# Another cost model in a kernel's planner, and value copies moved from DMA to GpSimd

## The chip, the core and the metric

One core of a Trainium2 chip runs the kernel as one program. The metric is device time in microseconds (us), median of the timed runs. An eight-byte-float input is read as pairs of 32-bit words; nothing is computed on the host.

## The reference, cut to what matters

Windowed attention with 32 global tokens (4 batches, 8 heads, 512 local tokens, head size 64, window 32), whose output is laid out as 2176 rows of 512, and then two feed-forward networks (512 to 2048 to 512) one after the other:

```python
s_ll = np.where(np.abs(pos[:, None] - pos[None, :]) <= 32, scale * q_l @ k_l.T, -1e9)
out_l = sm(concat([scale * q_l @ k_g.T, s_ll])) @ concat([v_g, v_l])
out_g = sm(scale * q_g @ concat([k_g, k_l]).T) @ concat([v_g, v_l])
x = rows(concat([out_g, out_l]))        # (2176, 512)
h = x @ w_in;   x = (h * cos(h)) @ w_out        # first network
h = relu(x @ w2_in);   out = (h * h) @ w2_out   # second network
```

The four weight matrices are eight-byte floats.

## The kernel before, in words

**Attention.** The work goes by 16 head pairs and 8 groups of two pairs (a group is half a batch). For a pair TensorE transposes keys and queries (`tk`, `tq`), forms windowed scores (`s`, L365), ScalarE takes the exponent (`pt`, L390), GpSimd gathers the part for the global keys (`pg`, L409), TensorE transposes the weights (`tw`, L418, and `tg`, L423) and multiplies them with the values (`o`, L441 and L456). Windows of 128 keys start at every 64th position, so the values are held twice: `va` as loaded, and `vb`, the same rows shifted by 64 partitions. In `copy_v` (L248) two DMAs per group on the queue of SyncE (SP), each of 64 partitions of 1024 numbers, make `vb` from `va`. All loads of attention stand on that queue too (`kn`, `qn`, `va`, `vgz`, `kgn`, `qgn`).

**Networks.** Each network is cut into blocks of the tokens (384, 384 or 320 columns twice) and into quarters of the hidden layer; a step is one block with one pair of hidden chunks. The first product of a step uses seven products of half-size blocks instead of eight (`PROD`, banks `ha`, `hb`, `he`), with sums of the inputs (`xr`, L681) and of the weights (`ws`, L160). Each operand is split in a high and a low part (`hi` by ScalarE, `lo` by L147 on GpSimd or VectorE), and three matmuls stand for one exact product. The weights are turned from eight-byte to four-byte floats first: two ScalarE or GpSimd instructions (L115 or L117, and L122), a shift and an OR on VectorE (L126, L131), a sum on GpSimd (L138). The second product of a step (`y`, L906) is added to the output tile `xt` by VectorE (L917), in its first round moved by VectorE or ScalarE (L921, L919). Inputs of the first product are stored to DRAM (`xs_B`, `xs_T`, L704) and read back (L709) for the later quarters.

**Planner.** Nothing above is issued in the order of the code. Every piece is an `Op` with the engines that can do it and a duration on each; the function walks over all `Op`s in a simulated time, gives each engine the ready one that is due first (`latest`), and emits the program in the order of the simulated starts. So a duration in the table is an instruction's place in the program. Ops on `Q` are DMAs of SP's queue. Each engine runs what it was given in that order, and one that waits holds all behind it. `opVG` makes an Op that VectorE or GpSimd can do; `port` names engines that the plan lets run only in turns; `beside[0]` is set from the first network's later preparations on; `made_early` are the preparations that may run beside attention; `nxt` counts the products that have been placed.

The lines that make a DMA and a shared operation in the plan:

```python
def opQ(kb, fn, *needs):
    return Op({"Q": kb / 330.0}, lambda e: fn(), *needs, lag=2.0)
def opVG(n, fn, *needs):
    o = Op({"G": d_g2(n), "V": d_v2(n)}, lambda e: fn(V if e == "V" else G), *needs)
    o.port = "GV"
```

Of the kernel before, what the change touches and what calls it, by code (L numbers as in the profile page):

```python
# [27 lines left out]
def kernel(  # L28
# [14 lines left out]
    nc = tc.nc  # L43
# [65 lines left out]
    def conv_u(q, m, c, on):  # L109
        t = raw[q, m, c]  # L110
        u = conv_to(q, m, c)
        tmp[q, m, c, 0] = u.bitcast(U32)
        h = t[:, :, 1].bitcast(F32)
        if on == "A":
            A.activation(u, h, AF.Copy, scale=2.0**-112)  # L115
        else:
            G.tensor_scalar(u, h, 2.0**-112, 1.0, op0=ALU.mult, op1=ALU.mult)  # L117
# [6 lines left out]
    def conv_v(q, m, c):  # L124
        u = tmp[q, m, c, 0]
        V.tensor_scalar(u, u, 3, None, op0=ALU.logical_shift_left)  # L126
# [118 lines left out]
                v_l[b, g, P * c - SG + r0 : P * c - SG + r1].rearrange("h p d -> p h d"),  # L245
            )

    def copy_v(gi):  # L248
        va, vb = VA[gi % 2], VB[gi % 2]
        nc.sync.dma_start(vb[0:64], va[64:128, 0:4])  # L250
        nc.sync.dma_start(vb[64:128], va[0:64, 1:5])

    def load_vg(b):

# [359 lines left out]
    load_qk("k", 1, 0, 2)  # L614
    load_qk("q", 1, 0, 2)
    load_vg(0)
    copy_v(0)
    load_qk("k", 1, 2, 2)
    load_qk("q", 1, 2, 2)
    for t in KT:  # L620
# [130 lines left out]
    def opV(d, fn, *needs):  # L751
        return Op({"V": d}, lambda e: fn(), *needs)

    def opG(d, fn, *needs):
        return Op({"G": d}, lambda e: fn(), *needs)

    def opVG(n, fn, *needs):
        o = Op({"G": d_g2(n), "V": d_v2(n)}, lambda e: fn(V if e == "V" else G), *needs)
        o.port = "GV"
        return o  # L760
# [1 line left out]
    beside = [False]  # L762

    def opQ(kb, fn, *needs):
        return Op({"Q": kb / 330.0}, lambda e: fn(), *needs, lag=2.0)

    class Ring:

# [304 lines left out]
    def conv(q, m, c):  # L1073
        j, free = raw_ring.next()
        k, cfree = cc_ring.next()
        RJ[q, m, c] = j, k
        ld = opQ(525.0, lambda: conv_load(q, m, c), *free)
        ld.lag += 0.0 if beside[0] else 4.0
        ld.raw = True
        if m:  # L1080
            w, wfree = wf1_ring.next()
            WJ[q, c] = w
        else:
            wfree = w_free["wf0"]
        u = Op({"G": 0.66, "A": 0.67}, lambda e: conv_u(q, m, c, e), ld, *wfree)
        s = opA(0.67, lambda: conv_s(q, m, c), ld, *cfree)
        v = opV(0.42, lambda: conv_v(q, m, c), u)
        o = opV(0.69, lambda: conv_o(q, m, c), s, u)
        v.port = o.port = "GV"
        raw_ring.free[j] = [o]  # L1090
        end = opG(1.25, lambda: conv_c(q, m, c), v, o)
        cc_ring.free[k] = [end]
        return end

# [40 lines left out]
    def opP(m, d, fn, *needs):  # L1135
# [3 lines left out]
        att_pe.append(o)  # L1139
        return o  # L1140

    def soft(fn, *needs):

        o = Op({"N": 0.0}, lambda e: fn(), *needs)
        o.soft = True
        return o
# [6 lines left out]
        for i in range(2):  # L1153
            q_in["k", 2 * g + i], q_in["q", 2 * g + i] = given(tk[i]), given(tq[i])
    q_in["v", 0] = given(12.0)
    q_in["vb", 0] = given(17.0)
    q_in["vg", 0] = given(15.0)
    q_in["kg", 0], q_in["qg", 0] = given(3.9), given(8.6)
    tring, TBANK = Ring(4), (0, 1, 2, 5)
# [15 lines left out]
    def load_kq(gi):  # L1175

        for w, free in (("k", kn_free), ("q", qn_free)):
            o = Op({"Q": 2.7}, lambda e, w=w: load_qk(w, gi), *free.get(gi - 2, []), lag=3.0)
            q_in[w, 2 * gi] = q_in[w, 2 * gi + 1] = o

    def load_vals(gi):
        o = q_in["v", gi] = Op({"Q": 3.1}, lambda e: load_v(gi), *va_free.get(gi - 2, []), lag=3.0)
        q_in["vb", gi] = Op({"Q": 1.2}, lambda e: copy_v(gi), o, *vb_free.get(gi - 2, []), lag=3.0)

    def load_vgz(b):
        q_in["vg", b] = Op({"Q": 1.9}, lambda e: load_vg(b), *vg_free.get(b - 2, []), lag=3.0)

    def tbank(*needs):
        k, free = tring.next()
# [223 lines left out]
    def join(*ops):  # L1413
        return Op({"N": 0.0}, lambda e: None, *ops)

    ORDER = (
# [12 lines left out]
    def att_graph():  # L1429
        mode[0] = "T"  # L1430
        for b in range(B):
            kg_ready[b], qg_ready[b] = join(), join()
        kg_b((0, 1))
        k_tr(0)
        q_tr(0)
        load_vals(1)
        load_vgz(1)
        for b in range(1, B):
            for w, dst, src in (("kg", kgn, k_g), ("qg", qgn, q_g)):
                q_in[w, b] = Op(  # L1440
                    {"Q": 0.45}, lambda e, b=b, dst=dst, src=src: load_small(dst, src, b), lag=3.0
                )
        for what in ORDER.split():
            name, i = what.split(":")
            DO[name](int(i))
# [86 lines left out]
    for o in allops:  # L1532
        set_latest(o)
    for o in made_early:
        o.latest -= 30
        if "Q" in o.on and hasattr(o, "raw"):
            o.latest -= 30

# [5 lines left out]
    def release(o):  # L1544
        if o.soft:
            o.at = max([x.start for x in o.needs]) + 1e-4
        else:
            p = "P" in o.on
            o.at = max([x.end + x.lag + (0.0 if p and x.eng == "P" else SEM) for x in o.needs], default=o.at)
        for e in o.on:  # L1550
            ready[e].append(o)

# [5 lines left out]
    def best(e):  # L1558
# [28 lines left out]
        if e in "VAG":  # L1587
# [20 lines left out]
                        return (min(g, min([max(f, y.at) for y in rest if y.att], default=g)), None) if g < t + 0.4 else (t, o)  # L1608
            if o.att:
                return t, o  # L1610
        if e in o.on and len(o.on) > 1 and e == "V" and o.latest > t + BIAS:
            can = [x for x in can if len(x.on) == 1 or x.latest <= t + BIAS]
            if not can:
                rest = [max(f, x.at) for x in ready[e] if len(x.on) == 1]
                g = max(min(free_at[x] for x in o.on if x != "V"), t)
                if g <= t + 0.5 or (rest and min(rest) < t + 0.3):
                    return (g + 1e-3, None) if not rest else (max(min(rest), t + 1e-3), None)
                return t, o
            o = min(can, key=lambda o: (o.latest, o.key))
        return t, o  # L1620

    port = [0.0]
    BIAS, LOOK, drift = -100, 1.0, [0.0]
    count = len(allops)
    while count:
        picks = [(b[0], e, b[1]) for e in ready for b in [best(e)] if b]
        t, e, o = min(picks, key=lambda x: (x[0], x[2] is None))
        if o is None:
            free_at[e] = max(t, free_at[e])
            continue  # L1630
        for x in o.on:
            if o in ready[x]:
                ready[x].remove(o)
        o.start, o.end, o.eng = t, t + o.on[e], e
        if e in o.port:

            o.end = port[0] = max(t, port[0]) + o.on[e]
        if e != "N":
            free_at[e] = o.end
        placed.append(o)  # L1640
        count -= 1
        if e == "P":
            if adone < len(att_pe) and o is att_pe[adone]:
                adone += 1
                drift[0] = o.start - o.latest
            elif nxt < len(order) and o is prods[order[nxt]]:
                nxt += 1
            else:
                jdone += 1
        for y in o.users:  # L1650
            missing[y.key] -= 1
            if missing[y.key] == 0:
                release(y)
# [40 lines left out]
```

## Time and profile before

| | |
|---|---|
| timed runs | 870.6 us median of 3 (867.48 to 871.53) |
| profiled execution | 863.49 us, its span 861.7 us |
| TensorE busy | 838.0 us of the span |
| VectorE, GpSimd, ScalarE busy | 613.8, 566.7, 529.8 us |
| mean granted TensorE clock | 0.997 |

Attention runs from the start to about 133 us, the first product of the first network starts at 130.9 us, and the last matmul ends near 857 us. TensorE has 23.7 us of the span in which it is not busy. Where these lie is in the rows that stand further down: a row of waits says which line stood still, what released it, the microseconds in total, how many times, and the longest.

### The profile page before, as it was taken

What the parts mean: (1) busy time and instruction counts of PE and PEld (TensorE: products, weight loads), DVE (VectorE), ACT (ScalarE), POOL (GpSimd) and SP (SyncE); (2) the same over time, 40 slices, a digit from 0 to 9 for tenths busy, and PEclk for the clock granted to TensorE, in tenths of its full rate; (3) what the DMA queues carried; (4) which work ended last, traced back from release to release, by engine and by line L of the source; (5) the groups of instructions that cost most, each with busy time, mean ns of one, the idle gap of its engine ahead of it and who ended that gap; (6) DMA issues with size and microseconds to landing.
All of it is one profiled execution on the core that took longest, in us unless ns stands there. A gap on an engine that the chain in (4) does not pass through costs nothing.

```text
span 861.7 us, 17103 instructions
## 1 busy us (share of the span) xinstructions
PE 838.0 (97%) x6100; PEld 778.2 (90%) x6100; DVE 613.8 (71%) x1379; ACT 529.8 (61%) x1264; POOL 566.7 (66%) x598
## 2 busy tenths in 40 slices
PE   8988998999989999999999998999999999999997
PEld 7867877999979999999999997999988989898886
DVE  6787978768687678767886779666766677454544
ACT  5898988877675656565665776656635454443331
POOL 3357689998897566657567999976866666441221
PEclk9999999999999999999999999999999999999999
DMA  9978974756684478548755555666774687446732
GB/s 187 213 188 203 227 228 139 276 183 235 221 332 140 157 281 306 172 131 306 250 196 172 223 201 199 220 233 231 276 250 170 239 282 218 140 161 239 224 118 80
DMA packets 134036, 181.99 MB, mean 211 GB/s; under 512 B 60736, under 2 KB 114496, under 8 KB 133952
## 3 DMA queue, kind: packets, MB, share of 16 engines
q1 hardware_dynamic: 130256, 179.73, 63.3%
q10 hardware_dynamic: 3696, 1.18, 0.6%
q8 instruction: 48, 0.79, 0.4%
q14 instruction: 36, 0.29, 0.1%
HBM read 141.03 MB, written 35.65 MB: 205 GB/s over the span
## 4 chain that ended last, share of the span: by engine, by line
PE 88%; DMA 3%; ACT 3%; DVE 3%; SPq 1%; issue 1%; POOL 1%; DVEq 0%; ACTq 0%
PE y L906 43%; PE hb L814 16%; PE he L814 10%; PE ha L814 10%; PE o L456 2%; PE s L365 2%; DMA raw<-in_moe_w_out_dram 1%; DMA vb<-va 1%; PE tw L418 1%; ACT pt L390 1%; PE o L441 1%; PE sg L500 1%; PE spin L648 1%; DVE pt L377 1%; DMA raw<-in_moe_w_in_dram 1%
## 5 line engine op out<-in xcount | busy, mean ns | idle before, releaser
L147 POOL TENSOR_TENSOR g<-cr,g 128x384 fp32r<-128x384 f32 (+1 forms) x192 | 199.4, 1047 | 140.3 <-ACT g L865 137.5
L917 DVE TENSOR_TENSOR xt<-y,xt 128x384 f32<-128x384 f32 (+2 forms) x287 | 170.0, 596 | 95.3 <-PE y L906 93.7
L906 PE MATMUL y<-g,wo 128*128 128x384 f32 (+1 forms) x1152 | 215.5, 326 | 0.0
L906 PE MATMUL y<-wo,g 128*128 128x512 f32 x816 | 209.2, 393 | 2.8 <-DVE wo L147 2.7
L906 PEld LDWEIGHTS y<-g,wo 128*128 128x128 f32 x1152 | 193.5, 188 | 0.0
L906 PEld LDWEIGHTS y<-wo,g 128*128 128x128 f32 x816 | 150.0, 188 | 28.3 <-DVE wo L147 3.5
L814 PE MATMUL hb<-xs,wi 128*128 128x384 f32 (+1 forms) x864 | 167.0, 328 | 4.6 <-ACT hb L825 4.1
L814 PEld LDWEIGHTS hb<-xs,wi 128*128 128x128 f32 x864 | 147.5, 188 | 10.7 <-ACT hb L825 4.5
L814 PE MATMUL ha<-xs,wi 128*128 128x384 f32 (+1 forms) x576 | 111.4, 328 | 2.3 <-DVE cr L857 2.3
L814 PE MATMUL he<-xs,wi 128*128 128x384 f32 (+1 forms) x576 | 110.7, 327 | 0.0
L865 ACT ACTIVATE g<-cr 128x384 fp32r<-128x384 f32 (+1 forms) x192 | 95.1, 503 | 22.8 <-DVE cr L857 22.2
L138 POOL TENSOR_TENSOR wf<-wf,cc 128x512 uint32<-128x512 uint32 x64 | 87.8, 1374 | 29.5 <-DVE wf L126 28.9
L814 PEld LDWEIGHTS ha<-xs,wi 128*128 128x128 f32 x576 | 98.5, 189 | 4.5 <-DVE cr L857 2.6
L814 PEld LDWEIGHTS he<-xs,wi 128*128 128x128 f32 x576 | 98.1, 188 | 4.0 <-DVE he L828 0.3
L131 DVE SCALAR_TENSOR_TENSOR cc<-raw,cc 128x512 uint32<-128x512 uint32 x64 | 63.2, 995 | 0.6 <-ACT cc L122 0.3
L851 ACT ACTIVATE cr<-cr,halfpi 128x384 f32<-128x384 f32 (+1 forms) x96 | 56.2, 593 | 9.2 <-DVE cr L846 8.2
L822 ACT ACTIVATE s<-hb 128x384 f32<-128x384 f32 (+1 forms) x48 | 22.7, 473 | 52.2 <-PE hb L814 50.4
L390 ACT ACTIVATE pt<-pt,st 128x160 f32<-128x160 f32 x128 | 53.1, 417 | 2.6 <-DVE st L377 2.0
L147 POOL TENSOR_TENSOR wi<-ws,wi 128x512 fp32r<-128x512 f32 x26 | 34.1, 1310 | 25.8 <-ACT wi L171 14.3
L122 ACT ACTIVATE cc<-raw 128x512 uint32<-128x512 uint32 x64 | 42.7, 669 | 12.9 <-DMA raw<-in_moe_w_in_dram 7.6
L828 DVE TENSOR_TENSOR he<-he,s 128x384 f32<-128x384 f32 (+1 forms) x48 | 26.0, 542 | 32.2 <-ACT s L822 32.1
L822 ACT ACTIVATE s<-he 128x384 f32<-128x384 f32 (+1 forms) x48 | 22.7, 473 | 41.7 <-PE he L814 41.3
(148 smaller groups left out, 1265.8 us busy)
## 6 DMA issues: line engine op xcount, KB each, us to landing
xs<-xs_T SPq DMA_DIRECT2D x48, 768.0 KB, 5.6
xs<-xs_B SPq DMA_DIRECT2D x36, 768.0 KB, 5.3
raw<-in_moe_w_in_dram SPq DMA_DIRECT2D x32, 512.0 KB, 6.0
raw<-in_moe_w_out_dram SPq DMA_DIRECT2D x32, 512.0 KB, 5.1
xs<-xs_T SPq DMA_DIRECT2D x24, 640.0 KB, 5.4
xs_T<-xs SPq DMA_DIRECT2D x16, 768.0 KB, 4.0
xs<-xs_B SPq DMA_DIRECT2D x18, 640.0 KB, 5.9
xs_B<-xs SPq DMA_DIRECT2D x12, 768.0 KB, 3.8
```

Of the source, the lines that this page charges most:

```text
L122: A.activation(v, raw[q, m, c][:, :, 0].bitcast(U32), AF.Copy, scale=2.0**-29)
L131: V.scalar_tensor_tensor(v, t[:, :, 1].bitcast(U32), 0x80000000, v, op0=ALU.bitwise_and, op1=ALU.bitwise_or,)
L138: G.tensor_tensor(u, u, v, op=ALU.add)
L147: eng.tensor_tensor(lo, x, hi.bitcast(F32), op=ALU.subtract)
L390: nc.scalar.activation(self.pt[hb][:, u, :], self.pt[hb][:, u, :], AF.Exp, bias=self.st[:, 0, 4 * hb + u : 4 * hb + u + 1], scale=-1.0, ac ...
L814: nc.tensor.matmul(out, lhsT=w[:, ws, c : c + P], rhs=xs[:, xh, kk, 0:n], start=start and k == 0, stop=k == 5, skip_group_check=True,)
L822: A.activation(self.sb[name], self.hold(bank_name), AF.Copy)
L828: V.tensor_tensor(self.hold(to), self.hold(bank_name), self.sb[name], op=ALU.add)
L851: A.activation(self.r[key], self.r[key], AF.Sin, bias=halfpi, scale=TWOPI)
L865: A.activation(GT[s, f][0][:, th * n : th * n + n], self.r[key], AF.Copy)
L906: nc.tensor.matmul(o, lhsT=l, rhs=r, start=k == 0, stop=k == 5)
L917: V.tensor_tensor(dst, y, dst, op=ALU.add)
```

## The change

The planner's table and rules are changed, and one kind of copy is done by another engine.

- `copy_v` can be done by GpSimd: two `tensor_scalar` instructions (times one) of 64 partitions by 1024. The plan does so for groups 0 to 3 (`GVB = 4`) at 2.6 us for both; groups 4 to 7 keep the DMAs.
- A DMA in the plan takes 0.53 us of issue on SP, one of 8 lanes, and its time on one shared way (`way`), and lands 2.2 us behind that; what it needs is taken 1 us later (`SLACK`). Before, it took its bytes over a rate on SP and landed after a fixed lag.
- With `beside[0]`, shared operations, the shift, the OR and the sums have longer durations, and VectorE's no longer wait their turn for GpSimd's.
- `made_early` is due 40 us ahead of its time instead of 30. `BIAS`, by which VectorE takes a shared operation only if it is due soon, is 6 us once 14 products are placed, and `EARLY` (-100, the old value) until then.

```diff
-    def copy_v(gi):
+    def copy_v(gi, eng="Q"):
         va, vb = VA[gi % 2], VB[gi % 2]
-        nc.sync.dma_start(vb[0:64], va[64:128, 0:4])
-        nc.sync.dma_start(vb[64:128], va[0:64, 1:5])
+        for dst, src in ((vb[0:64], va[64:128, 0:4]), (vb[64:128], va[0:64, 1:5])):
+            if eng == "Q":
+                nc.sync.dma_start(dst, src)
+            else:
+                copy(eng, dst, src)
...
     load_vg(0)
-    copy_v(0)
...
     def opVG(n, fn, *needs):
+        if beside[0]:
+            return Op({"G": 0.1 + n * 0.0026, "V": 0.2 + n * 0.002}, lambda e: fn(V if e == "V" else G), *needs)
...
     def opQ(kb, fn, *needs):
-        return Op({"Q": kb / 330.0}, lambda e: fn(), *needs, lag=2.0)
+        o = Op({"Q": 0.53}, lambda e: fn(), *needs)
+        o.dmas = [kb / 330.0]
+        return o
...
-        u = Op({"G": 0.66, "A": 0.67}, lambda e: conv_u(q, m, c, e), ld, *wfree)
+        u = Op({"G": 0.8 if beside[0] else 0.66, "A": 0.67}, lambda e: conv_u(q, m, c, e), ld, *wfree)
...
-        v = opV(0.42, lambda: conv_v(q, m, c), u)
-        o = opV(0.69, lambda: conv_o(q, m, c), s, u)
-        v.port = o.port = "GV"
+        v = opV(0.76 if beside[0] else 0.42, lambda: conv_v(q, m, c), u)
+        o = opV(1.0 if beside[0] else 0.69, lambda: conv_o(q, m, c), s, u)
+        v.port = o.port = "G" if beside[0] else "GV"
...
-        end = opG(1.25, lambda: conv_c(q, m, c), v, o)
+        end = opG(1.4 if beside[0] else 1.25, lambda: conv_c(q, m, c), v, o)
...
+    def dma(fn, n, kb, *needs):
+        o = Op({"Q": 0.53 * n}, fn, *needs)
+        o.dmas = [kb / 205.0] * n
+        return o
...
+        if gi < GVB:
+            q_in["vb", gi] = Op({"G": 2.6}, lambda e: copy_v(gi, e), o, *free)
+        else:
+            q_in["vb", gi] = dma(lambda e: copy_v(gi), 2, 256, o, *free)
...
+    GVB = 4
...
     for o in made_early:
-        o.latest -= 30
+        o.latest -= 40
...
+            if "Q" in o.on and o.needs:
+                o.at += SLACK
...
-        if e in o.on and len(o.on) > 1 and e == "V" and o.latest > t + BIAS:
-            can = [x for x in can if len(x.on) == 1 or x.latest <= t + BIAS]
+        if e in o.on and len(o.on) > 1 and e == "V" and o.latest > t + (BIAS if nxt >= 14 else EARLY):
+            can = [x for x in can if len(x.on) == 1 or x.latest <= t + (BIAS if nxt >= 14 else EARLY)]
...
-    port = [0.0]
-    BIAS, LOOK, drift = -100, 1.0, [0.0]
+    port, lanes, way = [0.0], [0.0] * 8, [17.0]
+    SLACK = 1.0
+    BIAS, EARLY, LOOK, drift = 6.0, -100, 1, [0.0]
...
+        if e == "Q":
+            f = t
+            for d in o.dmas:
+                f = max(f, lanes.pop(0)) + 0.53
+                way[0] = max(way[0], f) + d
+                lanes.append(way[0] + 2.2)
+            o.end, free = lanes[-1], f
...
-            free_at[e] = o.end
+            free_at[e] = free if e == "Q" else o.end
```

What this does to the program's order is shown at three places. First SP's queue in attention, from the copy of group 2 (`vb_95`) to the loads that follow the values of group 3 (`va_94`). Before:

```order
L250 DMA vb_95<-va_93 64x1024
L251 DMA vb_95<-va_93 64x1024
L97 DMA raw<-in_moe_w_out_dram 128x1024 x2
L233 DMA kn<-in_k_l_dram 128x4x64 x4
L240 DMA va_94<-in_v_g_dram 32x4x64
L243 DMA va_94<-in_v_l_dram 96x4x64
L243 DMA va_94<-in_v_l_dram 128x4x64 x3
L243 DMA va_94<-in_v_l_dram 32x4x64
L233 DMA qn<-in_q_l_dram 128x4x64 x4
```

The same place of the queue in the changed program, where the function's line numbers are 3 higher from here on:

```order
L233 DMA kn<-in_k_l_dram 128x4x64 x4
L233 DMA qn<-in_q_l_dram 128x4x64 x4
L97 DMA raw<-in_moe_w_out_dram 128x1024
L240 DMA va_94<-in_v_g_dram 32x4x64
L243 DMA va_94<-in_v_l_dram 96x4x64
L243 DMA va_94<-in_v_l_dram 128x4x64 x3
L243 DMA va_94<-in_v_l_dram 32x4x64
L97 DMA raw<-in_moe_w_out_dram 128x1024
L233 DMA qn<-in_q_l_dram 128x4x64 x4
```

The two copies are gone from the queue, the second weight load stands behind the values, and one key and one query load stand ahead of them.

Second, GpSimd's instructions where the copy of group 3 has come in (`vb_96`). Before, in the stretch from the second conversion sum of the first weights (L138):

```order
L138 TENSOR_TENSOR wf_855<-wf_855,cc 128x512
L117 TENSOR_SCALAR wf_1147<-raw 128x512
L409 TENSOR_SCALAR pg_117<-pt_109 128x2x2x32
L138 TENSOR_TENSOR wf_855<-wf_855,cc 128x512
L409 TENSOR_SCALAR pg_117<-pt_110 128x2x2x32
L285 TENSOR_SCALAR kT_101<-kT_101 128x7x64
```

In the changed program:

```order
L138 TENSOR_TENSOR wf_764<-wf_764,cc 128x512
L288 TENSOR_SCALAR vb_96<-va_94 64x1024 x2
L412 TENSOR_SCALAR pg_117<-pt_109 128x2x2x32
L138 TENSOR_TENSOR wf_764<-wf_764,cc 128x512
L412 TENSOR_SCALAR pg_117<-pt_110 128x2x2x32
L288 TENSOR_SCALAR kT_101<-kT_101 128x7x64
```

Both copies stand directly ahead of a gather `pg`, which is needed for a transpose on TensorE.

Third, VectorE in the first network, in the step that ends with the first use of a new pair of output weights (`wo`); the drains of `y` are L917, now L923, and the numbers tell the tiles apart. Before:

```order
L917 TENSOR_TENSOR xt_77<-y_4035,xt_77 128x384
L131 SCALAR_TENSOR_TENSOR cc_4045<-raw_4002,cc_4045 128x512
L126 TENSOR_SCALAR wf1_4075<-wf1_4075 128x512
L131 SCALAR_TENSOR_TENSOR cc_4072<-raw_4022,cc_4072 128x512
L126 TENSOR_SCALAR wf1_4087<-wf1_4087 128x512
L857 TENSOR_TENSOR cr_4060<-hd_4011,cr_4060 128x384
L917 TENSOR_TENSOR xt_77<-y_4064,xt_77 128x384
```

In the changed program, at the same product:

```order
L126 TENSOR_SCALAR wf1_4000<-wf1_4000 128x512
L863 TENSOR_TENSOR cr_4022<-ha_3904,cr_4022 128x384
L131 SCALAR_TENSOR_TENSOR cc_3998<-raw_3938,cc_3998 128x512
L852 SCALAR_TENSOR_TENSOR cr_4073<-he_3945,ck_4059 128x384
L126 TENSOR_SCALAR wf1_4024<-wf1_4024 128x512
L923 TENSOR_TENSOR xt_77<-y_4027,xt_77 128x384
L852 SCALAR_TENSOR_TENSOR cr_4091<-hd_4035,ck_4046 128x384
L863 TENSOR_TENSOR cr_4073<-he_3945,cr_4073 128x384
```

Four conversions in a row have become three with other work between them; the fourth, an OR, stands earlier.

## Rows read from the trace of the kernel before

**Rows 1.** The page's first part: busy us, share of the span, instructions of each engine.

```profile
PE 838.0 (97%) x6100; PEld 778.2 (90%) x6100; DVE 613.8 (71%) x1379; ACT 529.8 (61%) x1264; POOL 566.7 (66%) x598
```

**Rows 2.** Stretches: us, busy us of each engine (instructions), granted clock, DMA share, GB/s.

```profile
0.00:80.00 80.00, 71.92 (x1179) 60.69 (x1180) 61.55 (x307) 63.34 (x232) 37.71 (x78) 1.00 0.90 199
140.00:220.00 80.00, 77.51 (x464) 76.88 (x463) 59.51 (x103) 64.74 (x137) 71.51 (x69) 1.00 0.60 219
255.00:258.00 3.00, 3.00 (x10) 3.00 (x11) 2.45 (x4) 2.06 (x4) 3.00 (x3) 0.51 0.25 82
```

**Rows 3.** Waits of TensorE: line, releaser: us in total, times, longest.

```profile
PE hb L814 <- ACT hb L825: 4.1, 1, 4.1
PE o L456 <- DMA vb<-va: 3.1, 2, 2.7
PE y L906 <- DVE wo L147: 2.7, 2, 2.3
PE ha L814 <- DVE cr L857: 2.3, 1, 2.3
...
PE tqg L271 <- DMA qgn<-in_q_g_dram: 0.8, 1, 0.8
PE tog L588 <- ACT qgbd L281: 0.8, 1, 0.8
...
PE tq L316 <- DMA qn<-in_q_l_dram: 0.6, 3, 0.3
```

**Rows 4.** Timeline of TensorE: start, us, instruction; in brackets the idle time before.

```profile
68.49 0.24 PE L456 MATMUL o<-vb,tws 128*64 128x64 f32 x1 [2.67 <-DMA vb<-va]
...
143.10 1.34 PE L814 MATMUL ha<-xs,wi 128*128 128x384 f32 x6 [2.27 <-DVE cr L857]
...
254.89 2.15 PE L814 MATMUL hb<-xs,wi 128*128 128x384 f32 x6 [4.14 <-ACT hb L825]
256.83 1.97 PE L814 MATMUL ha<-xs,wi 128*128 128x384 f32 x6
258.64 1.21 PE L814 MATMUL hb<-xs,wi 128*128 128x384 f32 x6
259.69 1.20 PE L814 MATMUL he<-xs,wi 128*128 128x384 f32 x6
```

**Rows 5.** Timeline of SP's queue at the values of group 3.

```profile
54.15 3.47 SPq L243 DMA_DIRECT2D va<-in_v_l_dram  x5
...
63.09 0.51 SPq L250 DMA_DIRECT2D vb<-va  x1
63.65 0.60 SPq L251 DMA_DIRECT2D vb<-va  x1
```

**Rows 6.** Waits of SP's queue at the loads of output weights.

```profile
SPq L97 <- DVE cc L131: 76.3, 19, 19.3
```

**Rows 7.** GpSimd's groups, 0 to 130 us: count | busy us, mean ns | idle before.

```profile
L409 POOL TENSOR_SCALAR pg<-pt 128x128 f32<-128x128 f32 x32 | 9.7, 305 | 24.8 <-ACT pt L390 18.0 <-ACT tls L281 5.3 <-ACT xt L281 1.4
L285 POOL TENSOR_SCALAR kT<-kT 128x448 f32<-128x448 f32 x15 | 8.5, 566 | 17.2 <-ACT kT L281 10.8 <-DVE kT L283 6.4
...
L147 POOL TENSOR_TENSOR xs<-xr,xs 128x384 fp32r<-128x384 f32 x4 | 4.4, 1114 | 2.2 <-ACT xs L693 2.2
```

**Rows 8.** Timeline of VectorE around two stalls of the networks.

```profile
238.82 0.69 DVE L131 SCALAR_TENSOR_TENSOR cc<-raw,cc 128x512 uint32<-128x512 uint32 x1
...
248.04 1.70 DVE L131 SCALAR_TENSOR_TENSOR cc<-raw,cc 128x512 uint32<-128x512 uint32 x1
...
250.54 1.48 DVE L131 SCALAR_TENSOR_TENSOR cc<-raw,cc 128x512 uint32<-128x512 uint32 x1
251.95 1.48 DVE L126 TENSOR_SCALAR wf<-wf 128x512 uint32<-128x512 uint32 x1
...
527.65 2.90 DVE L147 TENSOR_TENSOR wo<-wf,wo 128x512 fp32r<-128x512 f32 x2
```

**Rows 9.** GpSimd's instruction beside the OR that starts at 248.04.

```profile
247.90 1.29 POOL L147 TENSOR_TENSOR wi<-wf,wi 128x512 fp32r<-128x512 f32 x1
```

**Rows 10.** VectorE's drains of 384 columns, 160 to 860 us.

```profile
L917 DVE TENSOR_TENSOR xt<-y,xt 128x384 f32<-128x384 f32 x112 | 61.1, 553 | 20.5 <-PE y L906 19.4
```

More of the change, by code (lines that the diff above doesn't have):

```diff
@@ L1077, in conv @@
         ld = opQ(525.0, lambda: conv_load(q, m, c), *free)
-        ld.lag += 0.0 if beside[0] else 4.0
+        ld.lag += 0.0 if beside[0] else 1.5
         ld.raw = True
@@ L1155 @@
     q_in["v", 0] = given(12.0)
-    q_in["vb", 0] = given(17.0)
     q_in["vg", 0] = given(15.0)
@@ L1177, in load_kq, with copy_vals @@
         for w, free in (("k", kn_free), ("q", qn_free)):
-            o = Op({"Q": 2.7}, lambda e, w=w: load_qk(w, gi), *free.get(gi - 2, []), lag=3.0)
+            o = dma(lambda e, w=w: load_qk(w, gi), 4, 128, *free.get(gi - 2, []))
             q_in[w, 2 * gi] = q_in[w, 2 * gi + 1] = o
     def load_vals(gi):
-        o = q_in["v", gi] = Op({"Q": 3.1}, lambda e: load_v(gi), *va_free.get(gi - 2, []), lag=3.0)
-        q_in["vb", gi] = Op({"Q": 1.2}, lambda e: copy_v(gi), o, *vb_free.get(gi - 2, []), lag=3.0)
+        q_in["v", gi] = dma(lambda e: load_v(gi), 6, 96, *va_free.get(gi - 2, []))
+        copy_vals(gi)
+    def copy_vals(gi):
+        o, free = q_in["v", gi], vb_free.get(gi - 2, [])
+        if gi < GVB:
+            q_in["vb", gi] = Op({"G": 2.6}, lambda e: copy_v(gi, e), o, *free)
+        else:
+            q_in["vb", gi] = dma(lambda e: copy_v(gi), 2, 256, o, *free)
     def load_vgz(b):
-        q_in["vg", b] = Op({"Q": 1.9}, lambda e: load_vg(b), *vg_free.get(b - 2, []), lag=3.0)
+        q_in["vg", b] = dma(lambda e: load_vg(b), 4, 32, *vg_free.get(b - 2, []))
     def tbank(*needs):
@@ L1435, in att_graph @@
         q_tr(0)
+        copy_vals(0)
         load_vals(1)
@@ L1439, in att_graph @@
             for w, dst, src in (("kg", kgn, k_g), ("qg", qgn, q_g)):
-                q_in[w, b] = Op(
-                    {"Q": 0.45}, lambda e, b=b, dst=dst, src=src: load_small(dst, src, b), lag=3.0
-                )
+                q_in[w, b] = dma(lambda e, b=b, dst=dst, src=src: load_small(dst, src, b), 1, 64)
         for what in ORDER.split():
```

## The prediction, made before the changed kernel was run

> **What bounds the kernel now.** I read the page's first part, then TensorE's waits, then its timeline at the longest of them, and last what the releaser had been doing. TensorE is busy 838.0 of 861.7 us [rows 1], so the change, which takes no matmul out, can win at most the 23.7 us in which TensorE stands still, and what the clock loses after a stall. The reader is to see in the waits that few rows hold most of it [rows 3]: 4.1 us for a bank seeded by ScalarE, 3.1 for the shifted values, 2.7 for output weights, 2.3 for the first step's cosine, and 2.2 for late attention loads and what follows from one (0.8 for `tqg`, 0.8 for the bank of `tog` that `tqg`'s evacuation holds, 0.6 for `tq`). That is 14.4 us. The rest is the start, the drain at the end and scattered tenths, which no part of the change touches.
>
> Each of these waits has a cause in another engine's order. The values: SP issued the five loads of group 3 by 57.6 us, its queue reached the two copies at 63.09, and 4.2 us after the second was issued (63.65 and 0.60) TensorE went on at 68.49 [rows 4, 5]. The seed at 254.89: VectorE ran four conversions in a row, of which one OR took 1.70 us and the last two instructions 1.48 each, while the same OR took 0.69 at 238.82 [rows 8]; the drain of a bank behind them came late, and so did ScalarE's seed. The output weights: VectorE finished the two low halves (2.90 us from 527.65) only when TensorE already stood at their first use [rows 8].
>
> **The shifted values, groups 0 to 3.** The stalls at vb belong to groups whose copies now go to GpSimd. In the new order the copy of group 3 stands on GpSimd some 13 TensorE groups ahead of its first use, and its loads stand behind one key load, one query load and one weight load, no longer behind two copies, two weight loads and a key load. The 3.1 us go. I take -3.1.
>
> Price of the copies: no row has a 64x1024 copy. GpSimd's nearest one-input rows are 128x128 in 0.305 us and 128x448 in 0.566 [rows 7]. Their slope, (0.566 - 0.305) / 320 = 0.0008 us an element, gives 0.566 + 576 x 0.0008 = 1.04 us; eight times the small one, 2.44 us, is the upper end. A pair takes 2.1 to 4.9 us, the eight copies 8 to 20. I take 1.04, since the larger row is the nearer. The cover is GpSimd's idle time: it works 37.7 of the first 80 us [rows 2], so 42 us are free. What shows is a pair standing ahead of a gather: behind it on GpSimd queue two `pg` and a `kT` copy, and TensorE's `tg` and scores wait for those. Bounds: nothing, to a whole pair of 2.1 us four times (8.4); the gathers wait 24.8 us in all for ScalarE's exponents [rows 7], some 0.8 us each, so much of a pair is hidden. I take +0.3.
>
> **SP's queue.** Four pairs of copies leave it (0.5 and 0.6 us of issue each [rows 5]), so each load behind them is issued 1.1 to 4.4 us earlier, and a wait of a copy for its values no longer holds the loads behind it. That is more than the longest of the late loads lacked (0.8 us). Of the 2.2 us [rows 3] I take -1.8; between 0 and -2.2 is possible. The attention-time stores of `xs` come earlier on SP, but over twenty TensorE groups behind the low halves that they read, so they hold nothing.
>
> **The burst at 254.89.** In the new order VectorE has three conversions there, with drains between, and over the surrounding 30 us of TensorE's work I count 17 GpSimd instructions where there were 28 and 46 of VectorE where there were 51. The 4.1 us go. The clock goes with them: from 255 to 258 the granted clock was 0.51, near the lower level of 1.2 GHz, where it was 1.00 before the stall [rows 2], and the first two products took 1.94 and 1.81 us from start to start, where the next took 1.05 [rows 4]. That is 1.65 us more. Together -5.8; the bounds are 0 and -5.8.
>
> **The output weights at 529.** The low halves of that pair stood 0.2 us of TensorE's work ahead of their first use in the old order and 3.7 us ahead in the new. An instruction of that kind took 1.45 us there (2.90 / 2 [rows 8]), so the wait should go. I take -2.3 of 2.7.
>
> **The start of the networks.** Here the change puts work in. Over the first 80 us of TensorE's work from the second step group on, the new order has 75 GpSimd instructions where there were 69, and 121 of VectorE where there were 106, nine of them drains that ScalarE had. GpSimd was busy 71.5 of the 80 us from 140 [rows 2]; six more at 1.11 us (the low half of 128x384 [rows 7]) are 6.7 us, which leaves under 2 us idle. VectorE gets 9 x 0.55 [rows 10] and 6 x about 1.1, 11.5 us on 59.5 [rows 2], which fits. The 2.3 us stall at 143.10 has its three conversions taken from ahead of the sine on ScalarE, but GpSimd now has two conversion sums ahead of the first low halves of `g`. I leave it as it is and add +2.0 for a GpSimd without slack. Bounds: -2.3, if the old stall goes and nothing comes, and +6.7 if nothing is hidden, with 1.7 more of slow clock.
>
> **Sum.** -3.1 + 0.3 - 1.8 - 5.8 - 2.3 + 2.0 = -10.7 us. Against the profiled execution's own 863.49 us (span 861.7 and 1.8 around it) that gives 852.8. The timed runs' median lies 7.1 us above that execution, with every engine's work the same, so I carry the difference over: 870.6 - 10.7 = 859.9. The forecast's own range is 854 to 866: all bounds at their good end give -16.1 (854.5), and with the copies' 2.1 us shown twice and 4 us at the start it is -4.8.
>
> **Rivals.**
> *GpSimd and VectorE take turns* (18%). The plan now lets both run at once in the networks, at longer durations. For it speaks the OR at 248.04: beside a sum on GpSimd that ran from 247.90 to 249.19 it ended at 249.74, 0.55 us behind that sum, as if it had begun only then [rows 8, 9]. Against it, that not every such pair is stretched so far. If they take turns, the six added low halves and sums on VectorE (6.6 us) and the six on GpSimd (6.7) share the 8.5 idle us from 140: 4.8 us late, with 1.7 of slow clock 6.5 in place of 2.0. Time 859.9 + 4.5 = 864.4.
> The Trainium skill's page "SBUF — State Buffer", section "SBUF: two separate sides", says that a VectorE operation with two SBUF inputs and a GpSimd operation that reads SBUF lock each other out for a whole instruction. By that rule this rival would hold, and the time be 864.4; the trace agrees at 248.04.
>
> *The bursts only move* (14%). The weights must be converted at some time, and a place that was quiet may stand still instead. For it: as many conversions as before, and GpSimd fuller early on. Against it: in the new order I find no place in the networks where over 2.2 us of work on two engines stands between two neighbouring products, and in the old one just the places of the two stalls. Then the 8.1 us of the two come back: 868.0.
>
> *A weight load holds the values* (12%, the slower side). A load of output weights now stands on SP directly ahead of the values of group 3. Such loads waited for VectorE's OR to free their buffer, 76.3 us in 19 waits, 4.0 in the mean and 19.3 at most [rows 6]. Behind it queue all value and query loads; GpSimd's copy then waits at the head of its queue, and the gathers behind it with TensorE's transposes. TensorE needs the values near 65.8 us (68.49 less 2.67 [rows 4]); less 2.1 for the copy and some 5.5 from the last issue to the copy (57.6 to 63.09 [rows 5]), they must be issued by about 58, which leaves about 8 us over their place in the new order: from a wait of 8 us on it costs. At 19.3 it costs 11.3 and slow clock of 1.7, and the 3.1 are not won: 859.9 + 3.1 + 13.0 = 876.0. Against it: the long waits of that row can lie in the networks, where the next quarter's weights are loaded early.
>
> **Chances and range.** Forecast 56%, rivals 18, 14 and 12. The range of 853 to 869 holds the first three; the fourth and a better end are left out. A measurement can tell about 0.5%, 4.4 us, from no change: faster is below 866.2. Faster: 54 of the forecast's 56, 15 of 18, 3 of 14, none of the last: 0.72. Slower (above 875.0): 1 of 14 and 10 of 12, 0.11. The same: 0.17.
>
> **What would show it.** TensorE's waits should have no row for vb, none over 1 us for a seed by ScalarE or for `wo`, and 0.5 granted nowhere in the networks. Eight rows of GpSimd, `vb<-va` 64x1024, of about 1.0 us, with `tg` not waiting for `pg` over 0.5 us. From 140 to 220 GpSimd should be near 78 us busy, and TensorE idle some 4.5 us there and in the ten before. I am wrong if the copies take over 2 us, if TensorE stands over 5 us between 135 and 220, or if a wait of a `raw` load in attention is followed by a late `va`.

## The result, and the profile after

The changed kernel took 860.71 us in the median of 4 runs (859.82 to 861.39), the kernel before 870.12 beside it (4 runs, 867.48 to 871.53): a ratio of 0.9895 [0.9869, 0.9921]. In two later sets of runs, on two chips, it took 860.81 and 861.24, and the kernel before 867.09 and 866.8 (ratios 0.9921 [0.9894, 0.9948] and 0.9933 [0.9919, 0.9948]). The forecast was 859.9, so the time came out as predicted. Much of the sum behind it did not, and the profile shows that at once: the execution profiled of after took 861.01 us, that of before 863.49, only 2.5 us more, where the sum said 10.7.

The page's first part and TensorE's waits, after ([rows 1, 3] of before):

```profile
PE 838.9 (98%) x6100; PEld 778.5 (91%) x6100; DVE 635.5 (74%) x1398; ACT 532.9 (62%) x1268; POOL 557.0 (65%) x583
```

```profile
PE o L459 <- DMA vb<-va: 4.2, 1, 4.2
PE y L912 <- POOL g L147: 3.8, 3, 2.1
PE tqg L274 <- DMA qgn<-in_q_g_dram: 1.3, 1, 1.3
PE hb L820 <- DVE hd L834: 1.1, 1, 1.1
...
PE tg L426 <- DMA kn<-in_k_l_dram: 0.6, 1, 0.6
```

The 4.1 us for the seeded bank are gone, and so are the 2.7 for `wo` and the 2.3 for the cosine. But the shifted values, which were to have no row, have the longest one, and a row of GpSimd's `g` is new. TensorE's timeline says where (start, us, instruction; in brackets the idle time before; [rows 4]):

```profile
63.33 0.27 PE L459 MATMUL o<-vb,tws 128*64 128x64 f32 x1
...
82.00 0.24 PE L459 MATMUL o<-vb,tws 128*64 128x64 f32 x1 [4.23 <-DMA vb<-va]
...
196.46 0.96 PE L912 MATMUL y<-g,wo 128*128 128x384 f32 x4 [1.44 <-POOL g L147]
...
254.62 1.20 PE L912 MATMUL y<-g,wo 128*128 128x384 f32 x6
...
526.00 1.77 PE L912 MATMUL y<-wo,g 128*128 128x512 f32 x4 [2.12 <-POOL g L147]
```

Group 3 starts with its shifted values at 63.33 where it did at 68.49 [rows 4], 5.2 us ahead. Group 4 starts at 82.00; before, it did so without a wait at 82.58:

```profile
82.58 0.27 PE L456 MATMUL o<-vb,tws 128*64 128x64 f32 x1
```

So 4.6 of the 5.2 us are given back by one wait at the first group whose copies are still DMAs. SP's queue shows why ([rows 5]):

```profile
49.58 3.97 SPq L243 DMA_DIRECT2D va<-in_v_l_dram  x5
...
64.51 5.65 SPq L243 DMA_DIRECT2D va<-in_v_l_dram  x5
70.25 2.03 SPq L233 DMA_DIRECT2D qn<-in_q_l_dram  x4
72.33 3.02 SPq L233 DMA_DIRECT2D kn<-in_k_l_dram  x4
75.45 1.87 SPq L262 DMA_DIRECT2D vgz<-in_v_g_dram  x4
77.36 1.19 SPq L252 DMA_DIRECT2D vb<-va  x2
```

Group 3's values are issued 4.6 us earlier than before (49.58 against 54.15); the forecast had 1.1 to 4.4. From group 4's values on, one entry of the queue follows the other. The five loads at 64.51 are mostly waiting: 3.5 of their 5.65 us go by until TensorE releases them (waits of SP's queue, 64.5 to 70.2 us):

```profile
SPq L243 <- PE o L459: 1.6, 1, 1.6
SPq L243 <- PE s L368: 1.1, 2, 0.6
SPq L243 <- PE tq L319: 0.8, 1, 0.8
```

Behind them stand 7 us of query, key and global-value loads, so group 4's copies leave the queue only at 77.36; TensorE goes on 3.5 us after their issue has ended.

The stretches of [rows 2], with two where the clock fell (us, busy us of each engine, granted clock, DMA share, GB/s):

```profile
0.00:80.00 80.00, 72.78 (x1208) 60.50 (x1208) 63.29 (x318) 66.27 (x245) 45.98 (x91) 1.00 0.85 192
80.00:86.00 6.00, 4.00 (x43) 3.92 (x44) 1.09 (x3) 1.66 (x5) 2.18 (x3) 0.72 1.08 243
140.00:220.00 80.00, 77.14 (x456) 75.68 (x455) 69.12 (x118) 63.99 (x132) 77.95 (x73) 1.00 0.60 215
255.00:258.00 3.00, 3.00 (x19) 3.00 (x18) 2.43 (x7) 1.35 (x4) 0.05 (x1) 1.00 0.56 164
527.00:530.00 3.00, 3.00 (x10) 2.76 (x10) 3.00 (x5) 1.75 (x3) 3.00 (x4) 0.53 0.95 389
```

Over the whole span TensorE now stands 20.3 us (859.2 less 838.9), where it stood 23.7, and it is busy 0.9 us longer: that makes the 2.5 us. From 255 to 258 the clock is at its upper level now (0.51 before). GpSimd is 77.95 us busy from 140 to 220; the forecast said near 78. The copies cost what their slope said (min/median/max ns, of the changed kernel's `vb`):

```profile
L288 POOL TENSOR_SCALAR vb<-va x8: 1038/1040/1364, 13.0 to 57.3; 64x1024 f32<-64x1024 f32 x8
```

### The profile page after: what moved, and what is told of

The parts are those of the page before. It is cut to its first block, busy times and chain, and to the rows that moved or that the text cites. A ratio compares the mean times of both kernels' runs of the same rounds, so it can differ in the third digit from the quotient of the medians.

```text
span 859.2 us, 17102 instructions
## 1 busy us (share of the span) xinstructions
PE 838.9 (98%) x6100; PEld 778.5 (91%) x6100; DVE 635.5 (74%) x1398; ACT 532.9 (62%) x1268; POOL 557.0 (65%) x583
## 4 chain that ended last, share of the span: by engine, by line
PE 85%; POOL 6%; DMA 3%; ACT 2%; issue 1%; SPq 1%; DVE 1%; ACTq 0%; POOLq 0%
PE y L912 42%; PE hb L820 15%; PE he L820 10%; PE ha L820 10%; POOL xs L147 2%; POOL g L147 1%; PE s L368 1%; PE o L459 1%; PE tw L421 1%; POOL wf L138 1%; DMA qn<-in_q_l_dram 1%; ACT pt L393 1%; PE sg L503 1%; POOL wo L147 1%; PE o L444 1%
## 5 line engine op out<-in xcount | busy, mean ns | idle before, releaser
L923 DVE TENSOR_TENSOR xt<-y,xt 128x384 f32<-128x384 f32 (+2 forms) x287 | 170.7, 596 | 102.5 <-PE y L912 100.6
L912 PE MATMUL y<-g,wo 128*128 128x384 f32 (+1 forms) x1152 | 217.8, 327 | 1.6 <-POOL g L147 1.6
L138 POOL TENSOR_TENSOR wf<-wf,cc 128x512 uint32<-128x512 uint32 x64 | 86.9, 1357 | 22.4 <-DVE wf L126 15.0
L147 POOL TENSOR_TENSOR wi<-ws,wi 128x512 fp32r<-128x512 f32 x27 | 36.2, 1339 | 24.1 <-ACT wi L171 12.7
L126 DVE TENSOR_SCALAR wf<-wf 128x512 uint32<-128x512 uint32 x64 | 49.6, 777 | 2.3 <-POOL wf L117 2.0
```

The lines of the kernel that those rows point to most:

```text
L138: G.tensor_tensor(u, u, v, op=ALU.add)
L147: eng.tensor_tensor(lo, x, hi.bitcast(F32), op=ALU.subtract)
L912: nc.tensor.matmul(o, lhsT=l, rhs=r, start=k == 0, stop=k == 5)
L923: V.tensor_tensor(dst, y, dst, op=ALU.add)
```

## The experiments

"Networks' part" is the longer durations (conversions, low halves), the 40 us for early work and the rule by which VectorE takes shared work that is due within 6 us (`BIAS`). "Attention's part" is the model of the transfers with the copies on GpSimd. To the model belongs a line that the diff above leaves out: the extra delay that the plan adds to a weight load beside attention goes from 4.0 to 1.5 us. The experiments ran in three sets, each on one chip (e1 to e4, e5 to e8, e9 to e12) with the kernel before beside it (866.85, 867.09 and 866.8 us).

| run | us, median (runs) | ratio to before | TensorE idle 15 to 130 us | 240 to 275 | 500 to 540 |
|---|---|---|---|---|---|
| e1_before | 866.9 (10) | 0.9993 [0.9972, 1.0015] | 8.9 | 3.7 | 2.8 |
| e2_networks | 864.01 (9) | 0.9957 [0.9934, 0.9979] | 12.2 | 0.0 | 0.4 |
| e3_copies | 865.28 (10) | 0.9968 [0.9944, 0.9991] | 5.6 | 7.9 | 2.4 |
| e4_gvb8 | 860.22 (4) | 0.9907 [0.9881, 0.9934] | 3.9 | 2.0 | 2.1 |
| e5_gvb0 | 865.05 (10) | 0.9969 [0.9951, 0.9986] | 11.7 | 0.0 | 2.1 |
| e6_attention | 872.11 (5) | 1.0054 [1.0035, 1.0072] | 5.2 | 7.1 | 2.4 |
| e7_after | 860.81 (4) | 0.9921 [0.9894, 0.9948] | 6.5 | 0.0 | 2.1 |
| e8_gvb6 | 856.16 (4) | 0.9875 [0.9845, 0.9905] | 5.7 | 0.0 | 2.1 |
| e9_bias | 867.93 (10) | 1.0007 [0.9992, 1.0022] | 7.2 | 5.1 | 1.9 |
| e10_durations | 858.45 (4) | 0.9903 [0.9884, 0.9922] | 7.5 | 0.0 | 1.2 |
| e11_gvb6 | 857.2 (5) | 0.9888 [0.9872, 0.9904] | 3.9 | 0.0 | 2.1 |
| e12_after | 861.24 (6) | 0.9933 [0.9919, 0.9948] | 7.6 | 0.0 | 2.1 |

The idle columns are the stretch less TensorE's busy time in the profiled execution. In the two executions of the result they are 7.5, 4.1 and 2.8 us for the kernel before, and 7.5, 0.0 and 2.1 for the changed kernel: attention as a whole stands as long as before.

**The kernel before, a second time** (no edit).

> The kernel before, unchanged, to see why its timed runs (870.1 us median) lie 7 us above the profiled execution that the prediction read (863.5). Theory: executions differ in how long the few stalls last; a new profile is 867 to 871 us long and its extra 4 to 8 us stand in TensorE's waits and in slow clock behind them. Rival: the extra lies outside the span or is spread over all instructions; then the new profile has the same waits (some 18 us) and either a span near 862 or matmuls that are longer everywhere. Ratio expected 1.00 by both.

Its profiled execution was a long one, 870.46 us (span 868.6), and the same order of instructions stood still for longer at the same places (TensorE's waits, then its timeline):

```profile
PE o L456 <- DMA vb<-va: 5.0, 3, 2.9
PE hb L814 <- ACT hb L825: 3.7, 1, 3.7
PE ha L814 <- DVE cr L857: 3.6, 1, 3.6
PE y L906 <- DVE wo L147: 2.7, 2, 2.3
PE tqg L271 <- DMA qgn<-in_q_g_dram: 1.6, 1, 1.6
```

```profile
148.13 2.29 PE L814 MATMUL ha<-xs,wi 128*128 128x384 f32 x6 [3.57 <-DVE cr L857]
```

The wait for the cosine is 3.6 us where [rows 3] have 2.3, and behind it six products take 2.29 us where they took 1.34 [rows 4]: the slow clock follows in one execution and not in the other. Of the 6.9 us between the two spans, 1.9 are idle time (25.6 us against 23.7); the other 5.0 are TensorE's own busy time (843.0 against 838.0), at a mean granted clock of 0.99 against 0.997. It was granted 0.97 from 15 to 130 us and 0.96 from 500 to 540, where the execution first profiled had 1.00. So the 7 us between the median and the execution first profiled are no constant beside the stalls: a part are these stalls, and more is slow clock. The 870.12 us of the result's set are on the long side themselves: in 24 runs beside this experiment the kernel before took 863.21 to 872.31, 866.85 in the median.

**The networks' part alone**, on the kernel before.

```
-        v = opV(0.42, lambda: conv_v(q, m, c), u)
-        o = opV(0.69, lambda: conv_o(q, m, c), s, u)
+        v = opV(0.76 if beside[0] else 0.42, lambda: conv_v(q, m, c), u)
+        o = opV(1.0 if beside[0] else 0.69, lambda: conv_o(q, m, c), s, u)
...
-    BIAS, LOOK, drift = -100, 1.0, [0.0]
+    BIAS, EARLY, LOOK, drift = 6.0, -100, 1, [0.0]
```

> The kernel before with the networks' part alone: longer durations, the shift and OR without turns, due times 40 us earlier and the new bias for VectorE; transfers and copies as before. Theory (the bursts carry the gain): the 4.1 us stall for the seed near 255 us goes, and with it the slow clock; 6 to 10 us faster than before (860 to 864). Rival (the transfers and copies carry it): under 3 us faster, 867 to 870.

The burst goes, as the theory said: no stall from 220 us on is above 1 us. The gain does not follow, and 2.8 us are what the rival allowed. Attention, which keeps the old costs of transfers, waits more for the values: 6.9 us in five waits.

**The copies on GpSimd alone**, with the old costs of transfers.

```
+        if gi < GVB:
+            q_in["vb", gi] = Op({"G": 2.6}, lambda e: copy_v(gi, e), o, *free)
```

> The kernel before with the copies of groups 0 to 3 by GpSimd alone, planned with the old model of transfers and the old durations. Theory (SP's queue is what attention waits for, and a gain at group 3 is given back at group 4): the waits at vb of groups 1 to 3 go, another of 2 to 4 us stands at a later group's copy, and the time is within 3 us of before. Rival (the copies are a gain of their own): no wait for a DMA over 1 us in attention and 3 to 5 us faster.

No wait for `vb` over 0.2 us, and 1.6 us won in the median. The wait that the theory expected at a later group is not there. Group 4, whose copies are still DMAs, starts at 77.71 with nothing waited for, 4.9 us ahead of the kernel before; its copies stand behind one load of keys and one of global values (SP's queue, then TensorE):

```profile
65.11 3.05 SPq L262 DMA_DIRECT2D vgz<-in_v_g_dram  x4
68.25 2.04 SPq L233 DMA_DIRECT2D kn<-in_k_l_dram  x4
70.34 1.18 SPq L252 DMA_DIRECT2D vb<-va  x2
71.63 3.37 SPq L233 DMA_DIRECT2D qn<-in_q_l_dram  x4
```

```profile
77.71 0.27 PE L459 MATMUL o<-vb,tws 128*64 128x64 f32 x1
```

In the changed kernel a load of queries stands ahead of them too, and they leave at 77.36 and not at 70.34. What attention won was lost elsewhere: a gather was late by 1.79 us at 110, and the burst stayed and was worse: 6.23 us, then the slow clock (timeline of TensorE).

```profile
256.25 2.29 PE L816 MATMUL hb<-xs,wi 128*128 128x384 f32 x6 [6.23 <-ACT hb L827]
258.33 2.12 PE L816 MATMUL ha<-xs,wi 128*128 128x384 f32 x6
```

**All eight groups copied by GpSimd** (`GVB = 8` in the changed kernel).

> The changed kernel with the copies of all eight groups by GpSimd (GVB 8 for 4). Theory: the 4.2 us wait at group 4 is SP's queue, whose copies stand behind vgz, kn and qn loads; without them it goes, and the time is 3 to 5 us under the changed kernel's (856 to 858). Rival: from 100 us on GpSimd is full with preparations, the four pairs (8.7 us) come out behind them, the gathers and the first products wait, and the time is the changed kernel's or up to 5 us more (861 to 866).

The wait of 4.2 us is gone, as the theory said, but the time is the rival's: all but the changed kernel's (860.22). TensorE now waits for gathers, 1.60 us at 117.87, and 1.97 at 135.20 for a sine. GpSimd's copies of the late groups lie where it prepares the networks; that they make these waits is argued and not shown.

**No group copied by GpSimd** (`GVB = 0` in the changed kernel).

> The changed kernel with the new model of the transfers and the new networks, but with all shifted copies on SP's queue as DMAs (GVB = 0). Theory A (SP's queue is what attention's loads and copies lack, so the copies cost there wherever the model puts them): the waits for vb come back at 4 to 7 us in sum, as in the kernel with the networks' part alone (6.9), and late loads with them; 863 to 865 us. Theory B (the old copies came late because the planner issued them badly, and the new model alone puts that right): waits for vb under 1.5 us, the time that of the changed kernel, 860 to 861.5 us.

Theory A. The waits for `vb` are 9.4 us in five, more than the 3.1 to 5.0 of the kernel before. Of them 2.0 are in group 0, whose copies the kernel before issues ahead of the plan and this one where the plan puts them. Beside e2, from which it differs by the model of the transfers and that placing, nothing is won (ratios 0.9969 and 0.9957, whose intervals overlap). The model of the transfers by itself puts nothing right; taking issues off SP's queue does.

**The attention's part without the networks' part** (the networks' lines of the second experiment set back in the changed kernel).

> The changed kernel without the networks' part: the model of the transfers and the copies on GpSimd, but the durations, the bias and the 30 us for early work of the kernel before. Theory A (the two parts add up; the networks' part was worth 2.9 us by itself): the stall for a bank seeded by ScalarE near 255 us is there, 3 to 6 us with a slow clock behind it, and ScalarE or VectorE holds the output weights at 530 for over 2 us; 863 to 865 us. Theory B (the bursts go by any new order, since they sit where the old plan put a conversion by chance): no stall of over 2 us between 220 and 540, 860 to 861.5 us.

Worse than either theory had it, and slower than the kernel before. In attention TensorE stands 5.2 us, less than the 7.5 and 8.9 of the kernel before's two profiled executions, but the networks lose more than that. VectorE at 258 to 265, and TensorE:

```profile
258.05 0.56 DVE L850 SCALAR_TENSOR_TENSOR cr<-he,ck 128x384 f32<-128x384 f32 x1 [0.20 <-ACT ck L847]
258.53 0.97 DVE L160 TENSOR_TENSOR ws<-wf,ws 128x256 f32<-128x256 f32 x1
259.42 2.27 DVE L131 SCALAR_TENSOR_TENSOR cc<-raw,cc 128x512 uint32<-128x512 uint32 x2
261.61 2.07 DVE L126 TENSOR_SCALAR wf<-wf 128x512 uint32<-128x512 uint32 x2
263.61 0.54 DVE L850 SCALAR_TENSOR_TENSOR cr<-hd,ck 128x384 f32<-128x384 f32 x1
```

```profile
264.67 2.29 PE L818 MATMUL he<-xs,wi 128*128 128x384 f32 x6 [4.84 <-DVE cr L861]
268.38 2.29 PE L818 MATMUL hb<-xs,wi 128*128 128x384 f32 x6 [1.42 <-ACT hb L829]
```

A sum of weights and four conversions in a row, 5.2 us on VectorE ahead of a step of the cosine; the plan had counted the four conversions at 0.42 and 0.69 (2.2 us), and they took 4.3 beside GpSimd. From 260 to 275 the granted clock was 0.66 in the mean. This is the burst of [rows 8] in another place. The two parts do not add up: -2.8 for the one, +5.0 for the other, and -5.6 to -6.3 for both.

This kernel differs from e3 by the model of the transfers alone, and it is the slower one (ratio 1.0054 [1.0035, 1.0072] against 0.9968 [0.9944, 0.9991], each to the kernel before beside it). Attention stands about as long in both (5.2 and 5.6 us), but here 3.13 us of it are a wait for `vb` in group 4, where e3 has none: it is the order that the new model makes which puts that wait there, and not the copies left on the queue as such. In neither pair of runs that differ by the model of the transfers (e3 and this one, e2 and e5) does the model win time. The changed kernel without it, with the networks' part and the copies on GpSimd, was not run.

**The rule for shared work, without the longer durations** (the kernel of the last experiment with `BIAS = 6`), and **the longer durations, without the rule** (the changed kernel with `BIAS = -100`).

> The new attention (model of the transfers, copies of four groups on GpSimd) with the old durations in the networks (that kernel took 872.1 us, with 7.2 us of waits for the cosine and a slow clock near 264), and of the networks' part only the new rule that lets VectorE take shared work due within 6 us. Theory A (VectorE's conversions planned at 0.42 and 0.69 us, where two took 1.0 and 1.1 each beside GpSimd, are what lets four stand in a row between two products): a stall of over 2 us with the slow clock stays somewhere between 220 and 540 us, 866 to 872 us. Theory B (it was GpSimd, which alone had all the low halves, that came late): no such stall, 860 to 862 us.

> The changed kernel with the longer durations and the earlier conversions of the networks, but without the rule that lets VectorE take shared work due within 6 us: GpSimd keeps all such work that is not overdue. Theory A (the longer durations keep the bursts out): no stall of over 2 us with a slow clock between 220 and 540 us beyond the known one for g near 526, 860 to 862 us. Theory B (the rule does it): GpSimd full at 140 to 220 us (over 78 of 80) and again from 500, waits for g or xs of over 4 us in sum there, 863 to 868 us.

Theory A in both, with a time under its range in the second. With the rule alone, a stall of 4.09 us and 2.29 us of slow products stand at 266.42; the time is that of the kernel before. With the durations alone there is none, and the kernel is faster than the changed one (857.25 to 860.15 against 860.61 to 862.02 in the same set): the waits for `g` at 196 and 526 are 0.42 us and none, with 0.40 for GpSimd's `wo` at the second place. Beside the longer durations the rule costs time, then. Beside the old ones it does not: without it the ratio to the kernel before is 1.0054 (e6), with it 1.0007 (e9), each in its own set. Why, the runs don't settle; one candidate is how the two engines run beside each other, VectorE first, then GpSimd, in the changed kernel ahead of the late `g`:

```profile
519.04 1.65 DVE L683 TENSOR_TENSOR xr<-xt 128x384 f32<-128x384 f32 x1
520.61 1.65 DVE L683 TENSOR_TENSOR xr<-xt,xr 128x384 f32<-128x384 f32 x1
522.18 1.65 DVE L147 TENSOR_TENSOR xs<-xt,xs 128x384 fp32r<-128x384 f32 x1
523.75 2.61 DVE L147 TENSOR_TENSOR xs<-xr,xs 128x384 fp32r<-128x384 f32 x2
```

```profile
518.66 1.61 POOL L138 TENSOR_TENSOR wf<-wf,cc 128x512 uint32<-128x512 uint32 x1
520.23 3.19 POOL L147 TENSOR_TENSOR wo<-wf,wo 128x512 fp32r<-128x512 f32 x2
523.38 2.57 POOL L147 TENSOR_TENSOR g<-cr,g 128x384 fp32r<-128x384 f32 x2
```

One instruction of each in turn, 1.57 us a pair. The low half that VectorE took over, 0.56 us at its shortest (below), costs GpSimd some 0.3 us of each of its own (1.61 and 1.60 where the shortest of these two took 1.26 and 1.28). But without the rule GpSimd's instructions there are stretched as well (1.29 to 1.74), and TensorE comes to that place 2.4 us later (the products `ha` of that step start at 524.67, against 522.22), so this is argued and not shown.

**Six groups copied by GpSimd** (`GVB = 6` in the changed kernel), and the changed kernel beside it.

> The changed kernel with the copies of six groups on GpSimd (GVB = 6), so that group 4's wait of 4.2 us goes and the last two groups, beside which GpSimd already works for the networks, stay with the DMAs. Theory A (the wait is a loss by itself): no wait for vb over 1 us, none of over 1 us for pg at 110 to 120, and 857 to 858.5 us. Theory B (what TensorE wins in attention it waits for GpSimd at the start of the networks, as with all eight groups, where 4.2 us won in one place came to about 0.5 us at the end): waits for pg, s, cr or g between 100 and 200 us grow by 3 us or more in sum, 859.5 to 861.5 us.

> Six groups' copies on GpSimd, a second time, beside the changed kernel. If its 856.2 us (four runs) were no chance: 855 to 858 us, and 3 us or more under the changed kernel beside it. If they were: 859 to 861 us, within 1.5 us of it.

> The changed kernel unchanged, a second time. If its waits follow from the order, the wait for vb in group 4 is there again with 3 to 5 us and that for g near 526 with 1.5 to 2.5, and the time is 860 to 861.5 us. If they are chance, as with part of the kernel before, the wait for vb is under 1.5 us and another wait stands elsewhere in attention, at the same time.

> The changed kernel, beside the one with six groups' copies. 860 to 861.5 us as three times before, with the wait for vb in group 4 at 4 to 5 us.

Theory A. In both profiled executions no wait for `vb`, in the second no late gather, and 857.2 us there (856.5 to 858.07) where the changed kernel took 861.24 (860.61 to 862.02): 4 us. It beats both kernels. That this is as much as the wait is chance in part: against the changed kernel beside it TensorE stands 3.7 us less from 15 to 130 us but 1.6 more from 130 to 240, and it is busy 1.8 us less in all. The waits of theory B do grow, to 4.7 us from 2.1 in sum (2.6, where it wanted 3): the start of the networks gives back 2.64 us for the cosine and then the slow clock, where the changed kernel waits 0.18 for it:

```profile
141.78 2.29 PE L820 MATMUL he<-xs,wi 128*128 128x384 f32 x6 [2.64 <-DVE cr L863]
```

The changed kernel itself had its wait in group 4 each time it was looked at (4.2, 4.6, 4.1 us, and 4.7 with the durations alone) and the one for `g` near 526 too (2.12, 2.14, 2.13): these follow from the order. Six groups without the rule for shared work was not tried.

## Why the prediction was right, and where it was not

**The sum against the profiled execution failed; the step that carried the median over made up for it, by luck.** "The timed runs' median lies 7.1 us above that execution, with every engine's work the same, so I carry the difference over" holds as if that difference were outside the stalls and their clock. It is not (first experiment), and TensorE's busy time was not the same either (843.0 against 838.0 us). The execution profiled of before was shorter than all four timed beside it; against it the change won 2.5 us, not 10.7, and after lies at its median where before lay 7 under it. Two errors of 8 and 7 us cancel. By the medians of the two later sets, with 14 and 17 runs of the kernel before, the gain is 5.6 to 6.3 us. Term by term, execution against execution:

- **Shifted values, -3.1:** wrong in its sum. Group 3's wait went, by the mechanism given; a wait of 4.2 us in group 4 took its place, and the granted clock of 0.72 from 80 to 86 us costs up to 1.7 more. I had looked at the four groups whose copies move and not at the next, whose copies stayed on SP's queue, where the new model of the transfers put 7 us of loads ahead of them; with the old model (e3) group 4 doesn't wait. The wait in group 4 is what e8 and e11 win back.
- **Copies, +0.3:** right; 1.04 us each, and no gather late in this execution (0.97 us at most in others with the same attention). One reading behind it is off: of the 24.8 us that the gathers wait, [rows 7] put 18.0 down to ScalarE's exponents and not all.
- **SP's queue, -1.8:** wrong. The late loads are 1.28, 0.57 and 0.36 us, 2.2 as before. The key load that is late at 60 us was issued from 56.24 on, 3.6 us earlier than before, and TensorE came to that transpose only 2.2 us earlier (59.41 against 61.63), so why it still waited is not shown. In two more executions of the changed kernel (e7, e12) they are 0 and 0.9, so this term differs by up to 2 us from one execution to the next.
- **The burst, -5.8:** right, stall and clock both. What I read from the order (three conversions in place of four, fewer instructions around) is the outcome; e9 and e10 show that the longer durations in the plan bring it about, and e6 that without them another attention can make the burst worse.
- **Output weights, -2.3:** their wait went, but 2.12 us for GpSimd's `g` stand in the same place, 3 us earlier in the trace, with a clock of 0.53 from 527 to 530 behind them, which costs up to 1.4 more (1.00 in e7, after the same stall). In this execution nothing is gained. I had counted the distance of VectorE's low halves and not what GpSimd had ahead of its own.
- **Start of the networks, +2.0:** right in sign, half the size. Idle from 130 to 240 us is 3.8 where it was 2.7, so +1.1. The old 2.3 us stall went; the longest wait now is the 1.44 us for `g` at 196.46. GpSimd's 77.95 us of 80 are as forecast, and TensorE stands 3.8 us from 130 to 220 where the prediction said 4.5.

**The rivals.** *Take turns:* its mechanism is real (519 to 526 us above), but the stretch from 130 to 240 us lost 1.1 us and not the 6.5 that it was to cost there. The Trainium skill's page "SBUF — State Buffer", section "SBUF: two separate sides", has a VectorE operation with two SBUF inputs and a GpSimd operation that reads SBUF lock each other out for whole instructions, and the trace agrees there: 1.57 us a pair. *The bursts only move:* not in the changed kernel, but in e6 and e9, to 264 and 266 us. *A weight load holds the values:* no; group 3's values were issued early, and GpSimd waited 2.57 us for them with no one behind it late.

**What was to show it.** Two signs failed: there is a row for `vb`, and 0.53 was granted in the networks. These held: no wait over 1 us for a seed by ScalarE or for `wo`, eight copies of about 1.0 us, GpSimd near 78.

## What to carry to other kernels

When transfers are taken off a full queue, look at the first user of that queue behind the ones you moved: in the changed kernel the gain ended there, and in e3, where fewer loads stood ahead of that user, it did not. Change one part of a planner's table at a time: the new costs of the transfers came with the copies, and no pair of runs shows that they win anything by themselves. A single profiled execution may be one of the short ones; before a sum is made against it, see where it lies in the spread of the timed runs, and do not carry the excess of the median over as a constant: here it was stalls and slow clock. Work handed to an engine that runs in turns with the first one (1.57 us a pair here) is not hidden, and a planner needs the durations measured side by side: with them in the plan the bursts went (e2, e10), without them they stayed (e3, e6, e9).

## What was not expected of the hardware

VectorE's conversions stretch beside GpSimd, its drains of the accumulators do not (changed kernel: min/median/max in ns, first and last start, and the widths of a sample):

```profile
L131 DVE SCALAR_TENSOR_TENSOR cc<-raw,cc x64: 640/998/1544, 40.3 to 715.1; 128x512 uint32<-128x512 uint32 x64
L126 DVE TENSOR_SCALAR wf<-wf x64: 407/698/1549, 51.4 to 713.2; 128x512 uint32<-128x512 uint32 x64
L147 DVE TENSOR_TENSOR xs<-xt,xs x13: 558/973/1651, 149.2 to 551.6; 128x384 fp32r<-128x384 f32 x8, 128x320 fp32r<-128x320 f32 x5
L923 DVE TENSOR_TENSOR xt<-y,xt x287: 474/558/692, 165.0 to 854.8; 128x512 f32<-128x512 f32 x60, 128x384 f32<-128x384 f32 x56, 128x320 f32<-128x320 f32 x28
```

L126 has one input and still goes from 0.41 to 1.55 us; L923, with one of two inputs in the accumulators, spreads from 0.47 to 0.69 over three widths. And a stall of the same 2.1 us at 526 was followed by the lower clock in two of three executions of the same kernel (0.53 over 527 to 530 here, 1.00 in e7), so whether a stall costs its clock too is not fixed by its length alone.
